# Block sums of v of batch 2: from TensorE products to GpSimd additions of a second load, with the list of steps from entry 270 to 660 in another order

## The chip, the cores and the metric

The kernel runs on one core of one Trainium2 chip. The time is the device time of one execution in microseconds; the median of three runs of the kernel before is 215.75 us (215.53 to 216.22). Differences of less than 0.3% can't be told from none with such runs.

## The reference

Two stages. The first is an attention over q, k, v of shape 4 x 8 x 768 x 64 (batch, head, position, width), in which each position sees its near neighbours and, in place of all the others, one summary per block of 32 positions: the maximum of k and the mean of v.

```python
k_sum = k.reshape(B, H, nb, block, D).max(axis=3)
v_sum = v.reshape(B, H, nb, block, D).mean(axis=3)
scores_l = scale * np.matmul(q, k.transpose(0, 1, 3, 2))      # kept where |i - j| < 16
scores_s = scale * np.einsum('bhsd,bhnd->bhsn', q, k_sum) + np.log(block)
a = softmax(concatenate([scores_l_m, scores_s], axis=-1))
out = np.matmul(a, concatenate([v, v_sum], axis=2))
```

The second is a two-layer network on the 3072 rows that come out (512 wide): h = x @ w_in (to 2048), g = h * clip(h + 3, 0, 6) / 6, y = g @ w_out.

The change concerns `v_sum`, the sums of 32 rows of v, of batch 2 alone.

## The kernel before, in words

**Tiles.** The 3072 rows are eight tiles s = 0 to 7 of 384 rows, two per batch. The *first product* of a tile and of one of 16 column groups ft (`F<s>x<ft>`, L695) is four TensorE products into one of three PSUM banks h0 to h2; ScalarE's relu (L699) and VectorE's gate (L700) turn it into 128 rows of g, and the gate sets the bank free for the third first product behind. The *second product* (`G<s><ts>x..`, L712) multiplies g with w_out in four parts; ScalarE or VectorE copies the result out (L244) and SyncE stores it.

**Attention, batches 1 to 3.** GpSimd issues the loads: k and q in four pieces of 192 KB each (`K<b><g>`, `Q<b><g>`, L336), v in two halves of 384 KB (`V<b>0`, `V<b>2`, L346), and for batches 2 and 3 a halo of v (`H<b>`, L355). Those of batch 2 go into the tile `first`, those of batch 3 into `kraw` and `qraw`. VectorE turns k and q (`w<b><p>`, L458 and L462; a turn reads all four pieces) and takes the block maxima (L470). The scores of a batch are four groups of 48 products (`s<b><u><half>`, L515) into both wide banks S0 and S1, each followed by two exponentials on ScalarE (L523) and two mask products on VectorE (L524). The values (`v<b><half><g>`, L652) need the scores' result, v and the block sums of v.

**Block sums of v** (`u<b+3>`, function `vsum`). For batches 1 and 2 TensorE makes them: 48 products of v with a 0/1 matrix `ind` (L558), a copy into `vs`, and four copies (`vspread2`, L244) that spread them over `vaug`, where the values read them. For batch 3 GpSimd makes them: v is loaded a second time in four pieces (`B3.0` to `B3.3`, `load_blocks`, L582), with the 32 rows of a block side by side in one partition, into the part of `first` that batch 2's k and q have left by then; then nine additions (L564): seven over 128x512 elements, two that halve what is left. The four copies are the same.

**Order.** Nothing is scheduled by the compiler: each engine works through its instructions in the order in which they are recorded, and the recording follows the string `ORDER` (L29 to L87), one entry per step: `u5.0` is step 0 of `vsum(2)`; `:A` and `:D` choose ScalarE or VectorE where both can do it. `Plan.issue` takes each entry in turn, gives it the PSUM bank or buffer that has been free longest, and records it. So an instruction that waits holds up whatever is listed later on its engine.

Of the kernel before, what the change touches and what calls it, by code (L numbers as in the profile page):

```python
# [9 lines left out]
F32 = mybir.dt.float32  # L10
# [29 lines left out]
v410.4:D =1 K12.0 v411.4:A F0x15.2 F0x14.0 F0x9.0 F0x14.1 F0x0.0 F0x9.1 F0x2.0 c.12:A Q1w0.0 F0x2.1 Q1w4.0 F1x4.0 F0x14.2  # L40
F1x4.1 F0x9.2 F1x14.0 w10.0 F1x14.1 F1x2.0 F1x2.1 Q1w1.0 F1x4.2 F0x2.2 F0x2.3 F0x0.1 Q1w2.0 F1x1.0 F1x14.2 F0x2.4 F1x8.0 F1x2.2
F1x1.1 F0x2.5 F1x8.1 F0x12.0 F0x0.2 F0x12.1 F1x1.2 F1x8.2 F0x0.3 F1x15.0 w10.1:A F0x12.2 F0x0.4 F0x0.5 F1x15.1 F1x9.0 F1x15.2
F1x9.1 F1x5.0 F1x9.2 w11.0 F1x5.1 F1x5.2 w10.2 q6.0 w11.2 w11.3:D w10.3:D q6.1:A q7.0 q7.1:A F1x7.0 F1x7.1 w11.1:A F1x7.2
F1x12.0 F1x12.1 F1x12.2 O0.0 G02x0.0 Q1w5.0 Q1w3.0 q4.0 q4.1:A q5.0 q5.1:A F1x6.0 F1x6.1 F1x6.2 O1.0 G02x0.1 s100.0 s100.1
s100.3 F1x3.0 w12.0 F1x11.0 F1x11.1 w13.0 w13.2 F1x3.1 F1x11.2 w12.2 w12.1:D O2.0 G02x0.2 s101.0 s101.1 O3.0 F1x10.0 G02x0.3
G02x0.4:A w13.3:D w13.1:A s101.3 F1x0.0 G00x0.0 G00x0.1 w12.3:D s100.2 s101.2 s100.4 V10.0 h100.0:D F1x10.1 h110.0:A F1x10.2
F1x3.2 s110.0 s110.1 s110.2 s101.4 s110.3 G00x0.2 G00x0.3 G00x0.4:A V12.0 u4.0 h130.0:D h120.0:A F1x0.1 u4.1:D u4.2:A u4.4:D
u4.3:D u4.5:D G02x0.5 G01x0.0 G01x0.1 G01x0.2 s110.4 F1x0.2 h111.0:A v100.0 v100.1 v100.2 h121.0:A v101.0 v101.1 v101.2 G01x0.3
G01x0.4:A K20.0 K21.0 K22.0 K30.0 K23.0 w21.0 F1x13.0 F1x13.1 F1x13.2 v100.3 v100.4:A w20.0 w21.3 G12x0.0 w21.2:A v101.3
v101.4:A V22.0 H2.0 h101.0:A w20.3 G12x0.1 G12x0.2 F2x2.0 F2x2.1 F2x11.0 F2x2.2 F2x11.1 F2x11.2 s111.0 w23.0 s111.3 F2x1.0  # L50
F2x1.1 F2x1.2 F2x3.0 F2x3.1 F2x3.2 F2x15.0 F2x15.1 F2x15.2 Q22.0 w23.3 G12x0.3 s111.1 G12x0.4:A F2x5.0 F2x5.1 h131.0:A F2x5.2
F2x6.0 G10x0.0 s111.2 w22.0 w22.3 s111.4 w23.4:A V20.0 H2.1:A K33.0 F2x13.0 F2x13.1 F2x13.2 G10x0.1 F2x6.1 F2x0.0 F2x0.1 F2x0.2
u5.0 u5.1:A u5.5:A F2x6.2 v110.0 v111.0 v111.1 v111.2 Q30.0 F2x4.0 F2x4.1 F2x4.2 Q21.0 Q23.0 Q20.0 w22.4:A F2x10.0 F2x10.1
F2x10.2 F2x12.0 F2x12.1 w20.1 F2x12.2 w22.2:A v110.1 w21.4:A Q33.0 Q32.0 G10x0.2 G01x0.5 G10x0.3 G10x0.4:A v110.2 F2x8.0 F2x8.1
w21.1 w20.2:A F2x9.0 w20.4:A F2x9.1 F2x9.2 u5.2:D F2x14.0 u5.4:D w23.2:A F2x8.2 v111.3 F2x14.1 v111.4:A G11x0.0 G11x0.1 u5.3:D
w22.1 v110.3 v110.4:A F2x7.0 F2x7.1 G11x0.2 F3x14.0 F3x14.1 F2x14.2 F2x7.2 F3x14.2 s200.0 s200.1 w23.1 w21.5:A s200.3 G11x0.3
F3x9.0 F3x9.1 F3x9.2 F3x8.0 F3x8.1 F3x8.2 F3x13.0 Q31.0 K31.0 s200.4 s200.2 G11x0.4:A G11x0.5 G12x0.5 s210.0 s210.3 s210.4
s210.1 s210.2 F3x4.0 F3x12.0 G22x0.0 F3x13.1 F3x13.2 H3.0 v201.0 K32.0 V32.0 w20.5:D F3x4.1 F3x4.2 V30.0 B3.0 B3.1 B3.2 B3.3
u6.0 u6.1 u6.2 u6.3 u6.4 u6.5 u6.6 u6.7 u6.8 G00x0.5 F3x12.1 v200.0 v200.1 F3x2.0 v201.1 v201.2 v201.3 G22x0.1 F3x0.0 F3x0.1
G22x0.2 G22x0.3 w23.5:A G22x0.4:A F3x12.2 v200.2 v200.3 v201.5 F3x1.0 F3x1.1 F3x1.2 s201.0 w31.0 G20x0.0 v201.4 F3x0.2 F3x2.1  # L60
s201.3 F3x2.2 F3x11.0 s201.1 G20x0.1 F3x5.0 F3x11.1 F3x3.0 F3x5.1 F3x11.2 w30.0 F3x5.2 v201.7 F3x15.0 G20x0.2 F3x15.1 F3x15.2
w30.3 F3x3.1 F3x3.2 w22.5:A w30.4:D s201.4 F3x6.0 F3x6.1 H3.1:A G20x0.3 G20x0.4:A F3x7.0 F3x10.0 G21x0.0 s211.0 F3x7.1 F3x10.1
s201.2 F3x7.2 s211.3 s211.1 F3x10.2 w32.0 F3x6.2 w32.3 s211.4 s211.2 w30.2:A G21x0.1 G21x0.2 G21x0.3 G21x0.4:A u6.12:A u6.11:A
u6.9:A w31.3 v211.0 v201.6 v210.0 v210.1 v210.2 w31.2:D v211.1 v210.3 v211.2 v211.3 G10x0.5 w31.4:D w33.0 G32x0.0 G32x0.1
# [17 lines left out]
F7x2.0 G62x0.1 F7x15.0 F7x2.1 F7x2.2 F7x15.1 F7x15.2 F7x0.0 G62x0.2 F7x0.1 G62x0.3 F7x7.0 F7x7.1 F7x0.2 G71x0.0 G62x0.4:D
G62x0.5 F7x7.2 F7x11.0 F7x11.1 G61x0.0 F7x11.2 F7x14.0 G71x0.1 G71x0.2 G71x256.0 G61x0.1 F7x14.1 F7x14.2 G71x0.3 G71x0.4:A
G72x0.0 G72x0.1 G71x0.5 G41x0.5 G70x0.0 G61x0.2 G61x0.3 G61x0.4:A G52x0.5 G70x0.1 G70x0.2 G72x0.2 G50x0.0 G50x0.1 G61x0.5
G50x0.2 G50x0.3 G72x0.3 G70x0.3 G50x0.4:A G50x0.5 G70x0.4:D G70x0.5 G60x0.0 G60x0.1 G60x0.2 G72x0.4:D G72x0.5 G60x0.3 G71x256.1
G71x256.2 G60x0.4:D G60x0.5 G71x256.3 G71x256.4 G71x384.0 G71x384.1 G71x384.2 G71x384.3 G71x384.4:D G71x384.5
# [76 lines left out]
def kernel(  # L163
# [40 lines left out]
    vrows = first[:].rearrange("p c x -> p (c x)")[:, 0:2 * BLK * D].rearrange("p (h t d) -> p h t d", h=2, t=BLK)  # L204
    quad = first[:].rearrange("p c x -> p (c x)")[:, 2 * BLK * D:2 * BLK * D + 16 * D].bitcast(F32).rearrange("p (h t d) -> p h t d", h=2, t=4)
# [343 lines left out]
    def vsum(b):  # L549
        plan.at(f"u{b + 3}")  # L550
        vs, i = Buf("vs"), b % 2
        if b < B - 1:
# [9 lines left out]
        else:  # L562
            def add(o, x, y):
                nc.gpsimd.tensor_tensor(o, x, y, op=ALU.add)  # L564

            def rows4(n):
                return vrows[:, :, 4 * n:4 * n + 4]
            op("POOL", "badd4", lambda: add(quad[:], rows4(0), rows4(1)), r=[("vb", c) for c in range(NP)], w=["part"], free=["part"])
            for n in range(2, BLK // 4):
                op("POOL", "badd4", lambda n=n: add(quad[:], quad[:], rows4(n)), w=["part"])  # L570
            op("POOL", "badd2", lambda: add(quad[:, :, 0:2], quad[:, :, 0:2], quad[:, :, 2:4]), w=["part"])
            op("POOL", "badd1", lambda: add(vs.slot[:].rearrange("p (h d) -> p h d", h=2), quad[:, :, 0], quad[:, :, 1]), r=["part"], w=[vs])
# [193 lines left out]
    for b in range(1, B):  # L766
# [18 lines left out]
        if b == B - 1:  # L785
            load_blocks(b)
# [53 lines left out]
```

## Time and profile before

| | us |
|---|---|
| median of the runs | 215.75 (215.53 to 216.22) |
| profiled execution, whole | 216.44 |
| its span, from the first to the last instruction | 214.7 |
| TensorE busy | 207.2 |
| VectorE busy | 161.1 |
| ScalarE busy | 137.2 |
| GpSimd busy | 61.5 |

The profiled execution is one more execution, and 0.69 us longer than the median; 1.7 us of it lie outside the span. Lines of the profile name the source line, the engine (PE is TensorE, PEld its weight loads, DVE VectorE, ACT ScalarE, POOL GpSimd, SP SyncE), the operation, the tiles as out<-in, the shape and the count. The rows of a timeline begin with start and duration in us; `[0.42 <-X]` is idle time of the engine before, and what ended it. A row of a group ends with busy time, mean duration in ns, and idle time before.

### The profile page before, as it was taken

To read this page: it belongs to the slowest core of one execution; us is meant where nothing else is said; L and a number is where in the kernel's file an instruction comes from. 1 tells how busy PE (TensorE), PEld (TensorE's weight loads), DVE (VectorE), ACT (ScalarE), POOL (GpSimd) and SP (SyncE) were. 2 spreads that over 40 slices of the span, in tenths; PEclk is the share of its full clock that TensorE was granted. 3 is DMA by queue.
4 is the path that set the end of the run, shared out by engine and by line. 5 is a ranking of instruction groups with operands and counts; after the bars stand their busy time and mean duration, and the time that the engine had idled before them with its cause. 6 is when DMAs were issued, how large, how long until landed. Compare 5 with 4: busy or idle time off the path is not lost.

```text
span 214.7 us, 5971 instructions
## 1 busy us (share of the span) xinstructions
PE 207.2 (97%) x2465; PEld 119.7 (56%) x2492; DVE 161.1 (75%) x311; ACT 137.2 (64%) x270; POOL 61.5 (29%) x79
## 2 busy tenths in 40 slices
PE   7998999999999999999999999999999999999994
PEld 7556566655555565555545555555555555564443
DVE  6886999899799999898899889887865555550021
ACT  3879978887888989765579696566346355520110
POOL 7968258905643237209700000000000000000000
PEclk9999999999999999999999999999999999999999
DMA  5999999999999999990234233113324300113123
GB/s 75 159 151 186 204 188 172 190 203 163 202 162 190 180 133 144 175 229 18 28 39 151 28 39 107 52 17 38 75 37 64 73 3 3 46 52 122 49 81 139
DMA packets 92043, 23.45 MB, mean 109 GB/s; under 512 B 82352, under 2 KB 88880, under 8 KB 92016
## 3 DMA queue, kind: packets, MB, share of 16 engines
q0 software_dynamic: 62608, 15.20, 74.8%
q1 hardware_dynamic: 29264, 7.80, 15.5%
q8 instruction: 19, 0.31, 0.6%
q10 hardware_dynamic: 144, 0.07, 0.1%
q14 instruction: 8, 0.07, 0.1%
HBM read 30.39 MB, written 6.29 MB: 171 GB/s over the span
## 4 chain that ended last, share of the span: by engine, by line
PE 88%; DMA 3%; ACT 2%; issue 2%; POOL 2%; DVE 1%; POOLq 0%
PE h L695 39%; PE o L712 32%; PE h L712 5%; DMA first<-in_q_dram 3%; PE S L652 3%; PE S L515 3%; ACT vaug L244 2%; POOL first L308 1%; PE S L695 1%; PE S L665 1%; PE S L492 1%; PE S L558 1%; PE S L442 1%; PE h L808 1%; DVE vaug L244 0%
## 5 line engine op out<-in xcount | busy, mean ns | idle before, releaser
L695 PE MATMUL h<-x,win 128*128 128x384 bf16 x500 | 91.4, 326 | 0.1
L700 DVE SCALAR_TENSOR_TENSOR g<-r,h 128x384 bf16<-128x384 f32 x125 | 65.8, 547 | 22.5 <-ACT r L699 19.8
L699 ACT ACTIVATE r<-h 128x384 f32<-128x384 f32 x125 | 58.4, 492 | 37.6 <-PE h L695 35.7
L712 PE MATMUL o<-wout,g 128*128 128x512 bf16 x309 | 78.0, 379 | 1.9 <-issue 0.8
L695 PEld LDWEIGHTS <-win 128*128 128x128 bf16 x512 | 48.7, 98 | 35.4
L712 PEld LDWEIGHTS <-g 128*128 128x128 bf16 x416 | 38.7, 98 | 37.4 <-issue 0.3
L523 ACT ACTIVATE at<-S 120x768 bf16<-120x768 f32 x24 | 18.6, 810 | 5.6 <-PE S L515 5.5
L244 ACT COPY ot<-o 128x512 f32<-128x512 f32 x17 | 10.0, 587 | 15.7 <-PE o L712 14.5
L524 DVE TENSOR_TENSOR at<-at,mask 96x768 bf16<-96x768 bf16 x24 | 12.6, 549 | 2.2 <-ACT at L523 1.8
L634 DVE TENSOR_TENSOR xn<-S,rc 128x768 bf16<-128x768 f32 x14 | 13.3, 950 | 0.3
L244 DVE COPY ot<-h 128x512 f32<-128x512 f32 (+1 forms) x3 | 1.6, 554 | 14.3 <-PE h L712 14.3
L346 POOL DMA_DIRECT2D vaug<-in_v_dram x10 | 11.8, 1192 | 0.0
L564 POOL TENSOR_TENSOR first<-first 128x512 f32<-128x512 f32 (+2 forms) x8 | 8.8, 1102 | 9.5 <-DMA first<-in_v_dram 8.9
L712 PE MATMUL h<-wout,g 128*128 128x128 bf16 (+2 forms) x80 | 11.4, 294 | 0.0
L244 ACT COPY vaug<-vaug 32x640 bf16<-32x640 bf16 (+3 forms) x20 | 10.6, 579 | 1.0 <-ACT qT L244 0.7
L470 DVE TENSOR_REDUCE red<-kaug 128x24 bf16<-128x768 bf16 x12 | 11.1, 939 | 0.1
L244 ACT COPY vaug<-vs 24x1536 bf16<-24x1536 bf16 x6 | 8.8, 1468 | 0.1
L808 PE MATMUL o<-idle 128*128 128x64 bf16 (+2 forms) x71 | 7.7, 286 | 1.1 <-DVE idle L290 1.1
L458 DVE STREAM_TRANSPOSE kaug<-kraw 128x768 bf16<-128x768 bf16 x8 | 8.1, 1026 | 0.3 <-PE S L515 0.3
L336 POOL DMA_DIRECT2D kraw<-in_k_dram x8 | 5.7, 724 | 8.4 <-DVE kaug L458 7.1
L652 PEld LDWEIGHTS <-at 120*64 120x64 bf16 x336 | 6.3, 111 | 3.2 <-issue 1.2
L515 PEld LDWEIGHTS <-kaug 32*128 32x128 bf16 x576 | 5.3, 92 | 4.6 <-issue 3.6
(114 smaller groups left out, 193.3 us busy)
## 6 DMA issues: line engine op xcount, KB each, us to landing
out_dram<-ot SPq DMA_DIRECT2D x19, 256.0 KB, 2.3
vaug<-in_v_dram POOLq DMA_DIRECT2D x6, 384.0 KB, 13.6
wout<-in_moe_w_out_dram POOLq DMA_DIRECT2D x4, 512.0 KB, 9.9
win<-in_moe_w_in_dram POOLq DMA_DIRECT2D x3, 512.0 KB, 10.6
kraw<-in_k_dram POOLq DMA_DIRECT2D x8, 192.0 KB, 12.5
x<-y SPq DMA_DIRECT2D x64, 24.0 KB, 2.0
first<-in_k_dram POOLq DMA_DIRECT2D x6, 192.0 KB, 12.7
first<-in_q_dram POOLq DMA_DIRECT2D x6, 192.0 KB, 11.5
```

Source lines behind the costliest of these rows:

```text
L244: {"ACT": nc.scalar.copy, "DVE": nc.vector.tensor_copy, "POOL": nc.gpsimd.tensor_copy}[eng](o, i)
L346: op("POOL", "dma128", lambda: nc.gpsimd.dma_start(out=o[BLK:WIN, a:z, 0:D], in_=rows[:, a:z]), w=[("v", b % 2, c) for c in range(lo, hi)] ...
L470: op("DVE", "max", lambda: nc.vector.tensor_reduce(red.slot[:], w[:, :, BLK:WIN].rearrange("p t (n c) -> p t n c", n=2), axis=AX.X, op=ALU ...
L515: nc.tensor.matmul(X[g // 2].slot[:, g % 2, i * QB:(i + 1) * QB], kaug[2 * u + m][rows, t], qT[rows, 2 * u + m, t * QB:(t + 1) * QB], star ...
L523: op("ACT", "exp", lambda a=a, e=e: nc.scalar.activation(a, X[e].slot[0:KEYS, :, 0:HALF], AF.Exp, scale=scl), r=[X[e]], w=[("at", p, half)])
L524: op("DVE", "masking", lambda m=m: nc.vector.tensor_tensor(m, m, mask[:, low(half):low(half) + HQ].unsqueeze(1).to_broadcast([WIN, 2, HQ, ...
L634: nc.vector.tensor_tensor(o, src[..., 0:D], r.unsqueeze(len(r.shape)).to_broadcast(list(o.shape)), op=ALU.mult)
L652: nc.tensor.matmul(X.slot[64 * c:64 * c + 64, i, m:m + D + 1], a[:, t * QB:(t + 1) * QB], vaug[b % 2][0:KEYS, h, t, 0:D + 1], start=True, ...
L695: nc.tensor.matmul(bank(h)[:, 0:HALF], w_in_sb[:, kt, cols], xt[s].slot[:, kt], start=(kt == 0), stop=(kt == NP - 1))
L699: op("ACT", "relu", lambda: nc.scalar.activation(r.slot[:], bank(h)[:, 0:HALF], AF.Relu, bias=0.5, scale=1.0 / 6.0), r=[h], w=[r])
L700: op("DVE", "gate", lambda: nc.vector.scalar_tensor_tensor(gt[s].slot[:, ft], r.slot[:], 1.0, bank(h)[:, 0:HALF], op0=ALU.min, op1=ALU.mul ...
L712: nc.tensor.matmul(o.slot[:, a:z], gt[s].slot[:, ft, ts * 128:(ts + 1) * 128], w_out_sb[:, ft, a:z], start=(ft == 0), stop=(ft == NFT - 1))
```

## The change

Batch 2's block sums are now made as batch 3's are: by GpSimd, from a second load of v. Since `first` still holds batch 2's k and q at that time, the load goes into a new tile `own`, whose unused rows GpSimd first sets to zero (`Z.0`). The 48 products, their bank and the copy out of it fall away for batch 2. Batch 1 keeps the products.

```diff
+    own = sb([128, 2 * BLK * D + 16 * D], BF16, "own")
+    lent = first[:].rearrange("p c x -> p (c x)")
+    vrows = {b: t[:, 0:2 * BLK * D].rearrange(...) for b, t in ((2, own), (3, lent))}
+    quads = {b: t[:, 2 * BLK * D:2 * BLK * D + 16 * D].bitcast(F32).rearrange(...) for b, t in ((2, own), (3, lent))}
...
     def vsum(b):
-        if b < B - 1:
+        if b < 2:
...
     def load_blocks(b):
+        if b == 2:
+            plan.at("Z")
+            op("POOL", "bzero", lambda: nc.gpsimd.memset(own[:, 0:2 * BLK * D].bitcast(F32), 0.0), w=[("vb", b, c) for c in range(NP)])
         plan.at(f"B{b}")
...
-               w=[("vb", c)], free=[(n, 0, g) for n in ("Kr", "Qr") for g in range(4)], size=48)
+               w=[("vb", b, c)], free=[(n, 0, g) for n in ("Kr", "Qr") for g in range(4)] if b == 3 else (), size=48)
...
-        if b == B - 1:
+        if b > 1:
             load_blocks(b)
```

The list gets twelve more entries, and those from about 270 to 660 stand in another order (the tail from `F4x8.0` on is as before, and so is the order of each engine but GpSimd ahead of `G02x0.0`). One line of it, before and after:

```diff
-F2x6.0 G10x0.0 s111.2 w22.0 w22.3 s111.4 w23.4:A V20.0 H2.1:A K33.0 F2x13.0 F2x13.1 F2x13.2 G10x0.1 F2x6.1 F2x0.0 F2x0.1 F2x0.2
+G10x0.3 v111.1 F2x5.1 F2x14.1 F2x14.2 Q33.0 F2x13.0 G12x0.5 F2x5.2 G10x0.4:A v110.1 u5.0 K33.0 F2x12.1 v111.2 F2x13.1 w20.4:A
```

TensorE, where the values of batch 1's second half begin (`at` are the masked scores, `vaug` v with its block sums, `h` the bank of a first product). Before:

```order
L695 LDWEIGHTS win
L695 MATMUL h_90<-x_99,win 128x384
L558 LDWEIGHTS ind
L558 MATMUL S_89<-vaug_76,ind 32x128
...
L652 LDWEIGHTS at_72
L652 MATMUL S_88<-vaug_77,at_72 64x65
```

After (lines behind the change are eight higher):

```order
L703 LDWEIGHTS win
L703 MATMUL h_91<-x_100,win 128x384
L660 LDWEIGHTS at_74
L660 MATMUL S_90<-vaug_78,at_74 64x65
L660 LDWEIGHTS at_74
```

The 48 pairs on `ind` are gone, and the values follow the first product.

GpSimd, from batch 2's q pieces to the end of its work. Before:

```order
L336 DMA first<-in_q_dram 32x24x128 x3
L336 DMA qraw<-in_q_dram 32x24x128 x3
L336 DMA kraw<-in_k_dram 32x24x128
L355 DMA vaug_77<-in_v_dram 32x95x64
L336 DMA kraw<-in_k_dram 32x24x128
L346 DMA vaug_77<-in_v_dram 64x48x64 x2
L582 DMA first<-in_v_dram 24x2x2048 x4
L564 TENSOR_TENSOR first<-first 128x512 x7
L564 TENSOR_TENSOR first<-first 128x2x128
L564 TENSOR_TENSOR vs_117<-first 128x128
```

After, the first chain of additions, on `own`:

```order
L567 TENSOR_TENSOR own<-own 128x512
L339 DMA kraw<-in_k_dram 32x24x128
L567 TENSOR_TENSOR own<-own 128x512
L339 DMA qraw<-in_q_dram 32x24x128
L567 TENSOR_TENSOR own<-own 128x512 x3
L339 DMA kraw<-in_k_dram 32x24x128
L567 TENSOR_TENSOR own<-own 128x512
L349 DMA vaug_78<-in_v_dram 64x48x64
L567 TENSOR_TENSOR own<-own 128x512
L590 DMA first<-in_v_dram 24x2x2048 x2
L567 TENSOR_TENSOR own<-own 128x2x128
L567 TENSOR_TENSOR vs_119<-own 128x128
```

and the second, on `first`:

```order
L590 DMA first<-in_v_dram 24x2x2048 x2
L339 DMA kraw<-in_k_dram 32x24x128
L358 DMA vaug_78<-in_v_dram 32x95x64
L567 TENSOR_TENSOR first<-first 128x512
L339 DMA qraw<-in_q_dram 32x24x128
L567 TENSOR_TENSOR first<-first 128x512 x6
L349 DMA vaug_78<-in_v_dram 64x48x64
L567 TENSOR_TENSOR first<-first 128x2x128
L567 TENSOR_TENSOR vs_118<-first 128x128
L339 DMA qraw<-in_q_dram 32x24x128
```

All loads stood ahead of the additions before. Now thirteen loads stand between additions or behind them, the last of them a piece of batch 3's q.

More of the change, by code (lines that the diff above doesn't have):

```diff
@@ L45 @@
[L45 to L48, printed above, removed]
@@ L53 @@
[L53 to L56, printed above, removed]
@@ L57 @@
[L57 to L64, printed above, removed]
@@ L82 @@
[L82 to L86, printed above, removed]
+F1x12.0 F1x12.1 F1x12.2 O0.0 G02x0.0 F1x10.0 F1x10.1 Q1w5.0 F1x10.2 Q1w3.0 O1.0 q4.0 q5.0 G02x0.1 F1x3.0 F1x6.0 q5.1:A q4.1:A
@@ new lines @@
+G20x0.1 F3x7.0 F3x0.0 w31.0 s201.3 F3x5.2 v201.4 v201.5 s201.1 s211.0 F3x7.1 u6.5 u6.6 F3x0.1 s211.3 F3x7.2 G20x0.2 s211.4
+G20x0.3 F3x0.2 F3x2.0 w32.0 F3x11.0 F3x1.0 G20x0.4:A G21x0.0 w31.3 F3x2.1 F3x2.2 v201.6 V30.0 u6.7 G21x0.1 G21x0.2 w31.2:A
+s201.2 G21x0.3 s211.1 v201.7 F3x6.0 w30.0 F3x11.1 F3x1.1 F3x11.2 u6.8 s211.2 G21x0.4:A s201.4 u6.11:A F3x10.0 v211.0 F3x1.2
+v210.0 F3x15.0 w32.3 F3x6.1 w30.3 F3x10.1 F3x6.2 u6.9:A F3x15.1 v211.1 F3x10.2 G32x0.0 G32x0.1 w33.0 F4x4.0 v210.1 u6.12:A
+F3x15.2 w32.2:A Q30.0 G32x0.2 G32x0.3 G32x0.4:A F4x15.0 v210.2 F4x14.0 v211.2 F4x4.1 F4x14.1 w30.4:D F4x15.1 G30x0.0 G30x0.1
@@ new lines @@
+F5x7.2 v311.1 F5x8.0 F5x8.1 F5x8.2 F5x10.1 F5x10.2 G40x0.2 F5x12.0 G40x0.3 G40x0.4:A G42x0.5 F5x15.0 F5x11.0 v310.3 v311.2
+v311.3 v311.7 F5x11.1 G32x0.5 G41x0.0 G41x0.1 G41x0.2 F5x11.2 F5x15.1 F5x15.2 F6x14.0 F5x12.1 F5x12.2 F6x14.1 F6x14.2 F6x12.0
+F6x12.1 F6x12.2 F6x9.0 F6x9.1 F6x9.2 G41x0.3 G41x0.4:A F6x10.0 F6x10.1 F6x7.0 F6x4.0 F6x4.1 F6x10.2 G52x0.0 F6x4.2 F6x7.1
+F6x7.2 F6x8.0 F6x8.1 F6x1.0 F6x8.2 F6x1.1 F6x1.2 F6x0.0 F6x0.1 F6x0.2 G52x0.1 F6x3.0 F6x11.0 F6x11.1 G52x0.2 F6x3.1 F6x3.2
+G52x0.3 G52x0.4:D F6x5.0 F6x5.1 F6x11.2 F6x2.0 F6x2.1 F6x5.2 F6x2.2 G51x0.0 F6x13.0 F6x13.1 F6x6.0 F6x15.0 G51x0.1 v311.6
@@ L87 @@
+G71x0.1 G71x0.2 G71x256.0 G61x0.1 F7x14.1 F7x14.2 G71x0.3 G71x0.4:A G72x0.0 G72x0.1 G71x0.5 G41x0.5 G70x0.0 G61x0.2 G61x0.3
+G61x0.4:A G52x0.5 G70x0.1 G70x0.2 G72x0.2 G50x0.0 G50x0.1 G61x0.5 G50x0.2 G50x0.3 G72x0.3 G70x0.3 G50x0.4:A G50x0.5 G70x0.4:D
+G70x0.5 G60x0.0 G60x0.1 G60x0.2 G72x0.4:D G72x0.5 G60x0.3 G71x256.1 G71x256.2 G60x0.4:D G60x0.5 G71x256.3 G71x256.4 G71x384.0
+G71x384.1 G71x384.2 G71x384.3 G71x384.4:D G71x384.5
 """
@@ L203 @@
     kraw, qraw = ([sb([128, NP * NB, BLK], BF16, f"{n}raw"), first[:, i * NP * NB:(i + 1) * NP * NB]] for i, n in enumerate("kq"))
-    vrows = first[:].rearrange("p c x -> p (c x)")[:, 0:2 * BLK * D].rearrange("p (h t d) -> p h t d", h=2, t=BLK)
-    quad = first[:].rearrange("p c x -> p (c x)")[:, 2 * BLK * D:2 * BLK * D + 16 * D].bitcast(F32).rearrange("p (h t d) -> p h t d", h=2, t=4)
+    own = sb([128, 2 * BLK * D + 16 * D], BF16, "own")
+    lent = first[:].rearrange("p c x -> p (c x)")
+    vrows = {b: t[:, 0:2 * BLK * D].rearrange("p (h t d) -> p h t d", h=2, t=BLK) for b, t in ((2, own), (3, lent))}
+    quads = {b: t[:, 2 * BLK * D:2 * BLK * D + 16 * D].bitcast(F32).rearrange("p (h t d) -> p h t d", h=2, t=4) for b, t in ((2, own), (3, lent))}
     at = [sb([128, 2, S], BF16, f"at{p}") for p in range(NP)]
@@ L564, in add @@
                 nc.gpsimd.tensor_tensor(o, x, y, op=ALU.add)
+            quad = quads[b]
             def rows4(n):
-                return vrows[:, :, 4 * n:4 * n + 4]
-            op("POOL", "badd4", lambda: add(quad[:], rows4(0), rows4(1)), r=[("vb", c) for c in range(NP)], w=["part"], free=["part"])
+                return vrows[b][:, :, 4 * n:4 * n + 4]
+            op("POOL", "badd4", lambda: add(quad[:], rows4(0), rows4(1)), r=[("vb", b, c) for c in range(NP)], w=[("part", b)])
             for n in range(2, BLK // 4):
-                op("POOL", "badd4", lambda n=n: add(quad[:], quad[:], rows4(n)), w=["part"])
-            op("POOL", "badd2", lambda: add(quad[:, :, 0:2], quad[:, :, 0:2], quad[:, :, 2:4]), w=["part"])
-            op("POOL", "badd1", lambda: add(vs.slot[:].rearrange("p (h d) -> p h d", h=2), quad[:, :, 0], quad[:, :, 1]), r=["part"], w=[vs])
+                op("POOL", "badd4", lambda n=n: add(quad[:], quad[:], rows4(n)), w=[("part", b)])
+            op("POOL", "badd2", lambda: add(quad[:, :, 0:2], quad[:, :, 0:2], quad[:, :, 2:4]), w=[("part", b)])
+            op("POOL", "badd1", lambda: add(vs.slot[:].rearrange("p (h d) -> p h d", h=2), quad[:, :, 0], quad[:, :, 1]), r=[("part", b)], w=[vs])
         for c in range(NP):
@@ L582, in load_blocks @@
             op("POOL", "dmarows", lambda c=c: nc.gpsimd.dma_start(
-                out=vrows[32 * c:32 * c + NB].rearrange("p h t d -> p h (t d)"),
+                out=vrows[b][32 * c:32 * c + NB].rearrange("p h t d -> p h (t d)"),
                 in_=v[b, 2 * c:2 * c + 2].rearrange("h (n t) d -> n h (t d)", t=BLK)),
-               w=[("vb", c)], free=[(n, 0, g) for n in ("Kr", "Qr") for g in range(4)], size=48)
+               w=[("vb", b, c)], free=[(n, 0, g) for n in ("Kr", "Qr") for g in range(4)] if b == 3 else (), size=48)
     xt, ys = {}, {}
```

55 lines of the change are left out of this document (31 added, 24 removed).

## Prediction

> **What bounds the kernel now.** I read the page's totals first, then the busy time by stretches, then the waits in the stretch that is laid out anew (44 to 121 us), then single instructions.
>
> ```profile
> span 214.7 us, 5971 instructions
> PE 207.2 (97%) x2465; PEld 119.7 (56%) x2492; DVE 161.1 (75%) x311; ACT 137.2 (64%) x270; POOL 61.5 (29%) x79
> DMA  5999999999999999990234233113324300113123
> 60.00:80.00 20.00, 19.66 (x288) 11.75 (x290) 19.28 (x32) 17.56 (x34) 7.25 (x10) 1.00 1.95 169
> 80.00:100.00 20.00, 19.68 (x249) 11.05 (x254) 18.66 (x33) 13.89 (x32) 9.54 (x11) 1.00 1.39 151
> 100.00:121.00 21.00, 20.72 (x239) 11.18 (x242) 19.27 (x36) 16.10 (x29) 5.74 (x6) 1.00 0.32 60
> PE o L712 <- issue: 0.6, 4, 0.2
> DVE g L700 <- ACT r L699: 2.6, 6, 0.7
> ```
>
> The columns of the stretches are TensorE, its weight loads, VectorE, ScalarE and GpSimd. TensorE works 60.06 of the 61 us from 60 to 121; what it waits for between 44 and 121 us adds up to 0.6 us. So TensorE's work is the time, at a granted clock of 1.00. But VectorE is close behind: 57.21 of the same 61 us, and 96% from 60 to 80. It waits 2.6 us for ScalarE. The DMA row is full to slice 18 (97 us). So whatever leaves TensorE is gain at once, as long as neither VectorE nor a load becomes late by more than the little that is spare.
>
> **What leaves TensorE.** The block sums of batch 2 in the timeline, with what stands around them:
>
> ```profile
> 75.54 0.81 PE L695 MATMUL h<-x,win 128*128 128x384 bf16 x4
> ...
> 76.28 0.68 PEld L558 LDWEIGHTS <-ind 96*32 96x32 bf16 x48 [0.32 <-DMA qraw<-in_q_dram]
> 76.29 0.85 PE L558 MATMUL S<-vaug,ind 96*32 96x128 bf16 x48
> ...
> 76.64 1.47 DVE L700 SCALAR_TENSOR_TENSOR g<-r,h 128x384 bf16<-128x384 f32 x3
> 77.07 0.90 PEld L652 LDWEIGHTS <-at 120*64 120x64 bf16 x48
> ...
> 77.19 0.27 ACT L244 CAST vs<-S 128x128 bf16<-128x128 f32 x1 [0.25 <-PE S L558]
> ...
> 78.01 2.12 PE L695 MATMUL h<-x,win 128*128 128x384 bf16 x12
> ```
>
> From the first weight load of the sums to that of the values behind them: 77.07 - 76.28 = 0.79 us. All of it goes, with ScalarE's copy of the sums (0.27 us, hidden). The short idle of the weight loads ahead of such a group (0.32 us here) stays: it belongs to the change from a first product to a group of another tile shape. The old order has 14 such changes in the stretch and the new one 14 as well, since the values now follow a first product directly. The number of products, transposes, scores and values on TensorE is the same. So the term is **-0.8 us**. What the other order makes of the 0.94 us that TensorE does not work between 60 and 121 I put at nothing, with bounds: all of it may go, or as much may come. One new wait I can name: the second score group of batch 1 now has one first product fewer between it and the group before, whose two banks it takes over.
>
> **GpSimd's side.** It gets a memset, four loads and nine adds, ahead of the nine it has.
>
> ```profile
> L564 POOL TENSOR_TENSOR first<-first 128x512 f32<-128x512 f32 (+2 forms) x8 | 8.8, 1102 | 9.5 <-DMA first<-in_v_dram 8.9
> L336 POOL DMA_DIRECT2D first<-in_q_dram x4 | 2.9, 717 | 4.7 <-DMA vaug<-in_v_dram 4.3 <-issue 0.3
> L346 POOL DMA_DIRECT2D vaug<-in_v_dram x4 | 5.4, 1342 | 0.0
> L582 POOL DMA_DIRECT2D first<-in_v_dram x4 | 2.6, 678 | 1.3 <-DVE qT L462 1.3
> L252 POOL MEMSET ident<- 128x128 bf16 x1 | 0.2, 224 | 0.0
> 59.79 1.12 POOL L336 DMA_DIRECT2D qraw<-in_q_dram  x1 [0.75 <-DMA first<-in_k_dram]
> 65.36 0.71 POOL L336 DMA_DIRECT2D first<-in_q_dram  x1 [2.69 <-DMA vaug<-in_v_dram]
> 78.65 1.33 POOL L355 DMA_DIRECT2D vaug<-in_v_dram  x1 [5.35 <-PE S L652]
> 96.23 9.36 POOL L564 TENSOR_TENSOR first<-first 128x512 f32<-128x512 bf16 x8 [8.95 <-DMA first<-in_v_dram]
> 105.67 0.46 POOL L564 TENSOR_TENSOR vs<-first 128x128 bf16<-128x128 f32 x1
> DMA to landing us min/median/max: 11.1/11.1/11.1
> DMA to landing us min/median/max: 6.3/6.3/6.3
> first<-in_v_dram POOLq DMA_DIRECT2D x4, 192.0 KB, 9.3
> ```
>
> The first landing row is of the load issued at 65.36, the second of the halo load of batch 3 (issued at 78.65, after GpSimd had waited 5.35 us and the queue had run nearly empty). The memset has 2048 elements a row against 128 for 0.224 us: between 0.2 and 3.6 us, beside a full queue, free.
>
> Fourth new load landed: before, the load of 65.36 landed at 76.5, and by then the queue had brought all k, q and v pieces of batch 2 and three pieces of batch 3; now the fourth new load has ahead of it 960 KB less (one v half of 384 KB, three pieces of 192) and, itself included, 768 KB more. At 169 GB/s that is 75.3 us; if the new loads, whose rows are long, take only the 0.6 us a piece at which the old ones were issued, 73.0. Adds: a chain of nine is 96.23 to 106.13 = 9.9 us. Between them the new order puts three loads of 0.72, one of 1.34 and two of 0.68: 4.9 us. So the sums of batch 2 stand at 87.8 to 90.1. They are needed when VectorE spreads them, and the next chain goes on behind: two more issues, a landing of 6.3 to 9.3 us, 9.9 us of adds with loads of 0.72 and 1.34 between: end of the sums of batch 3 at 107 to 112, then the last q load of batch 3, landing at 113 to 121. The needs:
>
> ```profile
> 91.03 1.21 DVE L700 SCALAR_TENSOR_TENSOR g<-r,h 128x384 bf16<-128x384 f32 x2 [0.55 <-ACT r L699]
> 112.71 0.59 ACT L244 COPY ot<-o 128x512 f32<-128x512 f32 x1 [0.49 <-PE o L712]
> 120.65 1.02 DVE L462 STREAM_TRANSPOSE qT<-qraw 128x768 bf16<-128x768 bf16 x1
> ```
>
> The first spread of batch 2 now stands behind the gate of 91.03 (done at 91.58), with 0.5 us less VectorE work ahead by the order and the mean durations of the groups: 91.1, or 90.3 where TensorE is 0.8 earlier. ScalarE spreads batch 3 behind the output copy of 112.71, with 3.5 us less ahead: about 109.8. The first turn of q of batch 3, at 120.65, has 2.9 us less ahead and TensorE 0.8 earlier: 117.0. For the first chain I take the middle, 89.0. Behind it I take the short landing, because the DMA row is far from full after slice 18: 89.0 + 0.7 + 6.3 = 96.0 for the last load, + 9.9 + 0.72 + 1.34 = 107.9 for the sums of batch 3, + 6.3 = 114.2 for the q load. So the three needs are met with 1.3, 1.9 and 2.8 us to spare, and the cost taken is **0**; at the upper ends the last one is 4.4 us late.
>
> **VectorE's side.** It has the same number of instructions and nearly the same work, in 0.8 us less: of its 3.8 us of idle time from 60 to 121, 3.0 are left. What is spare before TensorE notices is read above: the three gates that begin at 76.64 end at 77.18 to 78.11, and the products that take their banks start at 78.01, 78.66 and 79.31: 0.8 to 1.2 us. Cost taken: 0.
>
> GpSimd and VectorE may also stop each other. The trace shows a little of it:
>
> ```profile
> 84.87 1.12 DVE L244 COPY vaug<-vs 24x1536 bf16<-24x1536 bf16 x2
> L582 POOL DMA_DIRECT2D first<-in_v_dram x4: 603/609/892, 84.6 to 86.7; - x4
> L524 DVE TENSOR_TENSOR at<-at,mask 96x768 bf16<-96x768 bf16 x16 | 8.3, 548 | 0.5 <-ACT at L523 0.3
> 107.46 1.01 DVE L524 TENSOR_TENSOR at<-at,mask 96x768 bf16<-96x768 bf16 x2
> ```
>
> One of four load issues takes 0.89 instead of 0.61 us, the one beside VectorE's copies: 0.3 us. Beside the adds (96 to 106) VectorE had no mask product; those at 107.46 come after them. In the new order two mask products fall into the second chain, none into the first. If each stands through a whole add of 1.16 us, that is 2.3 us of VectorE. The Trainium skill ("SBUF — State Buffer", section "Who interferes with whom") states just this: a VectorE instruction with two SBUF inputs contends with a GpSimd instruction that reads SBUF, and the later one waits for the whole of the other. By that rule the sum would be up to 1.3 us higher (2.3 less the 1.0 spare); no row here shows it for adds.
>
> **The sum.** The profiled execution took 216.44 us, 1.7 beyond its span; the median of the runs shown is 215.75. Both lose the same 0.8: 215.64 for a run like the profiled one, and **215.0** for the median, which I give.
>
> **The rivals.**
> - *VectorE takes over.* For it: 96% in one stretch. Against: its waits are for ScalarE, whose work falls. The 0.8 us come back as waits for gates: 215.4 to 216.2, say 215.8. Chance 0.23.
> - *GpSimd's chain is late.* For it: one q load that was issued at 59.8 us is now GpSimd's last instruction but the end, behind eighteen adds and the landings they wait for. VectorE, in order, stands at the turn of q, with the gates behind it. At the upper ends 4.4 us late, less 1.0 spare, 3.4 reach TensorE: 215.0 + 3.4 = 218.4. It costs something from 3.8 us beyond my value on (2.8 + 1.0), and turns the sign past the measure from 5.2. Chance 0.13.
> - *Masks stand behind adds*, as above: 216.3. Chance 0.05.
> - *The new layout also takes the rest of TensorE's idle time*: -0.8 - 0.9 gives 214.1. Chance 0.12.
>
> **How the numbers follow.** The forecast (214.7 to 215.4) has 0.47. A measurement of this kernel tells about 0.3%, 0.65 us: below 215.10 counts as faster, above 216.40 as slower. Faster: 0.12 and three quarters of 0.47, so 0.47. Slower: nearly all of 0.13 and a little of the rest, 0.14. The same: 0.39. The range 214.2 to 216.7 leaves out half of the best case and most of the late chain.
>
> **What would show it.** In the profile after: no 48 products on the indicator of batch 2; TensorE's waits between 44 and 121 us still under 1 us, and the last first product of tile 3 about 0.8 us earlier. Right on GpSimd: the first chain ends by 90 us, the second by 109, and no VectorE or ScalarE wait names GpSimd or a q load. Wrong: a VectorE wait on the q load of batch 3 near 117 us; a ScalarE wait on the sums near 110; mask products of more than 1 us between 100 and 108; or VectorE without idle time and TensorE's products waiting for gates.

## The result, and the profile after

| | before | after |
|---|---|---|
| median of the executions, us | 215.93 (215.53 to 216.61, 20) | 218.02 (215.98 to 221.79, 20) |
| ratio, with its 95% interval | | 1.0061 (1.0042 to 1.0081) |
| profiled execution, us | 216.44 | 217.09 |
| its span, us | 214.7 | 215.4 |
| TensorE busy, us | 207.2 | 205.4 |

Slower by 0.6%, or 1.3 us, where 0.8 us less was forecast. The ratio leaves out the seven slowest executions of the changed kernel, of which more at the end; the profiled one has a granted clock of 1.0.

The page of the changed kernel: totals, and TensorE's row of slices.

```profile
span 215.4 us, 5887 instructions
PE 205.4 (95%) x2416; PEld 118.3 (55%) x2444; DVE 159.5 (74%) x310; ACT 135.8 (63%) x270; POOL 74.7 (35%) x93
PE   7998999999999999999995999999999999999994
```

TensorE does less work, as it should (2416 products on record against 2465), but the row has a 5 in slice 22 (113 to 118 us). Before, that slice was full:

```profile
PE   7998999999999999999999999999999999999994
```

The waits of TensorE between 44 and 121 us (total, times, longest), which before came to 0.6 us:

```profile
PE h L703 <- DMA x<-y: 2.5, 1, 2.5
PE o L720 <- issue: 0.6, 4, 0.2
PE S L660 <- DVE vaug L247: 0.2, 1, 0.2
```

One new wait of 2.5 us, and it is for a transfer that the prediction never mentions. In the timeline, the weight loads (PEld) of the first second product, of tile 3's last group, of tile 4's first product, and of the place from which the two lists are alike again:

```profile
43.35 0.69 PEld L720 LDWEIGHTS <-g 128*128 128x128 bf16 x4
...
111.67 1.55 PEld L720 LDWEIGHTS <-g 128*128 128x128 bf16 x8
116.16 0.45 PEld L703 LDWEIGHTS <-win 128*128 128x128 bf16 x4 [2.93 <-issue]
...
121.37 1.94 PEld L703 LDWEIGHTS <-win 128*128 128x128 bf16 x12
```

TensorE's products of tile 4 in the same timeline, with the wait ahead of them:

```profile
116.19 0.81 PE L703 MATMUL h<-x,win 128*128 128x384 bf16 x4 [2.46 <-DMA x<-y]
```

The same weight loads in the kernel before (tile 4's first product aside):

```profile
44.18 0.69 PEld L712 LDWEIGHTS <-g 128*128 128x128 bf16 x4
...
113.78 1.19 PEld L712 LDWEIGHTS <-g 128*128 128x128 bf16 x7
...
120.71 1.94 PEld L695 LDWEIGHTS <-win 128*128 128x128 bf16 x12
```

And there, tile 4's first products:

```profile
117.25 1.95 PE L695 MATMUL h<-x,win 128*128 128x384 bf16 x11
```

Read these in pairs. At 44 us the changed kernel is 0.83 us ahead, ahead of anything that the change touches: that is how two executions differ (over the twelve kernels traced here, of both orders, this load starts between 43.24 and 44.62 us). At the last group of tile 3 it is 113.78 - 111.67 = 2.11 us ahead, so 1.28 us were gained in between: the forecast's 0.8 and some 0.5 more. This pair can't put the 0.5 down to the other order: one of the kernels below ("The same loss made in the kernel before", the loads alone), in which TensorE has the order of before, does the same stretch in 69.20 us, the kernel before in 69.60. Then comes the wait, and from 121 us on the kernel is 121.37 - 120.71 = 0.66 us behind. Gain of 1.28, loss of 2.77, net 1.49 us later; the ratio says 1.3.

**What the transfer is.** A tile's x, which its first products read, is put together by SyncE: VectorE turns the values (`y`, L679), and 16 small transfers of 24 KB move it into place (`x<-y`, L685; L677 before). The instructions of that line between 99 and 118 us are the 16 moves of tile 4. Before:

```profile
L677 SPq DMA_DIRECT2D x<-y x16: 617/618/1710, 100.2 to 111.3; - x16
DMA to landing us min/median/max: 2.0/2.0/3.4
```

After, with who waited for them:

```profile
L685 SPq DMA_DIRECT2D x<-y x16: 617/620/1446, 101.0 to 112.2; - x16
  PEld L703: 2.9, 1
  PE h L703: 2.5, 1
DMA to landing us min/median/max: 2.0/3.3/5.3
```

The first row gives the issue of one (ns, least, median, most) and the starts of the first and the last. One is issued every 0.7 us, so the last leaves SyncE at 111 to 112 us in both kernels. What differs is the landing: 2.0 us in the middle before, 3.3 after. For the wait only the last one counts: issued at 111.3 us it landed 2.8 us later, near 114.1, before; issued at 112.2 it landed 3.8 us later, near 116.0, after. So of the 1.9 us between them 0.9 is a later issue and 1.0 a longer landing. And the first product that needs it stood at 117.25 us before, 3 us behind the last landing (114.1 in the trace); now, listed behind two parts of tile 3's last group instead of four, and with TensorE 1.28 us ahead, it could start at about 113.7 us.

**GpSimd's side.** Its two chains in the timeline of the changed kernel (first and last of the first chain, first of the second, the last v half, the end of the second chain, the last q piece):

```profile
73.61 1.34 POOL L567 TENSOR_TENSOR own<-own 128x512 f32<-128x512 bf16 x1 [5.15 <-DMA own<-in_v_dram]
...
87.46 0.46 POOL L567 TENSOR_TENSOR vs<-own 128x128 bf16<-128x128 f32 x1
...
96.71 1.15 POOL L567 TENSOR_TENSOR first<-first 128x512 f32<-128x512 bf16 x1 [5.58 <-DMA first<-in_v_dram]
...
106.05 1.36 POOL L349 DMA_DIRECT2D vaug<-in_v_dram  x1
...
108.25 0.46 POOL L567 TENSOR_TENSOR vs<-first 128x128 bf16<-128x128 f32 x1
108.64 0.73 POOL L339 DMA_DIRECT2D qraw<-in_q_dram  x1
```

On VectorE, the first spread of batch 2 and the first turn of q of batch 3:

```profile
91.28 0.56 DVE L247 COPY vaug<-vs 24x1536 bf16<-24x1536 bf16 x1
...
117.35 1.00 DVE L465 STREAM_TRANSPOSE qT<-qraw 128x768 bf16<-128x768 bf16 x1
```

Nothing here is late: sums of batch 2 at 87.9 us, those of batch 3 at 108.7, and neither the spread at 91.28 nor the turn of q at 117.35 has idle time ahead of it. But see the last two loads, a v half of 384 KB at 106.05 and a q piece of 192 KB at 108.64. Before, they were issued at 82.0 and 59.8 us, ahead of the moves; now they are issued among them (101 to 112 us), and land 6.9 and 5.7 us later, near 113.0 and 114.3. The moves issued up to 106.6 us land in 2.0 to 2.9 us, those issued from 107.2 on in 3.8 to 5.3.

### The profile page after: what moved, and what is told of

Read it like the earlier page. It is cut to its first block, busy times and chain, and to the rows that moved or that the text cites. A ratio compares the mean times of both kernels' runs of the same rounds, so it can differ in the third digit from the quotient of the medians.

```text
span 215.4 us, 5887 instructions
## 1 busy us (share of the span) xinstructions
PE 205.4 (95%) x2416; PEld 118.3 (55%) x2444; DVE 159.5 (74%) x310; ACT 135.8 (63%) x270; POOL 74.7 (35%) x93
## 4 chain that ended last, share of the span: by engine, by line
PE 83%; SPq 5%; DMA 4%; ACT 2%; issue 2%; DVE 2%; POOL 0%; POOLq 0%
PE h L703 37%; PE o L720 28%; PE h L720 5%; SPq L685 5%; PE S L518 2%; PE S L660 2%; DMA first<-in_k_dram 2%; DMA x<-y 2%; PE o L816 1%; DVE vaug L247 1%; ACT vaug L247 1%; PE S L703 1%; PE S L673 1%; PE S L495 1%; PE h L816 1%
## 5 line engine op out<-in xcount | busy, mean ns | idle before, releaser
L703 PE MATMUL h<-x,win 128*128 128x384 bf16 x500 | 91.1, 326 | 2.5 <-DMA x<-y 2.5
L527 DVE TENSOR_TENSOR at<-at,mask 96x768 bf16<-96x768 bf16 x24 | 13.6, 584 | 2.0 <-ACT at L526 1.6
L567 POOL TENSOR_TENSOR own<-own 128x512 f32<-128x512 f32 (+2 forms) x8 | 9.1, 1135 | 5.4 <-DMA own<-in_v_dram 5.1
L247 ACT COPY vaug<-vaug 32x640 bf16<-32x640 bf16 (+2 forms) x18 | 9.3, 575 | 0.7 <-ACT qT L247 0.7
```

The source lines that it names most:

```text
L247: {"ACT": nc.scalar.copy, "DVE": nc.vector.tensor_copy, "POOL": nc.gpsimd.tensor_copy}[eng](o, i)
L527: op("DVE", "masking", lambda m=m: nc.vector.tensor_tensor(m, m, mask[:, low(half):low(half) + HQ].unsqueeze(1).to_broadcast([WIN, 2, HQ, ...
L703: nc.tensor.matmul(bank(h)[:, 0:HALF], w_in_sb[:, kt, cols], xt[s].slot[:, kt], start=(kt == 0), stop=(kt == NP - 1))
```

## The experiments

The theory: *moves against loads, and an early product*. Two loads that GpSimd now issues late share the DMA engines with SyncE's moves of tile 4's x, and tile 4's first product is listed where it can no longer stand a late landing. The rivals: the GpSimd additions themselves (through memory or through VectorE), or the other order on TensorE. All ratios are to the kernel before, on the same chip.

### The two loads ahead

GpSimd issues both ahead of the second chain.

```diff
-v201.0 H3.0 F3x14.2
+v201.0 H3.0 V30.0 Q30.0 F3x14.2
...
-v201.6 V30.0 u6.7
+v201.6 u6.7
...
-w32.2:A Q30.0 G32x0.2
+w32.2:A G32x0.2
```

> The last v half and the last q piece of batch 3 are issued ahead of the second chain of additions instead of inside and behind it; all else as in the changed kernel. Theory 'moves': the 16 transfers that bring tile 4's x together land late because these two loads run beside them (last landing 115.9 us, 3.8 us after its issue, where 2.0 is usual); then the last one lands near 114.2, TensorE's wait ahead of tile 4's first product falls from 2.8 to about 1.0 us, and the time falls by 1.8 us against the changed kernel. Rival 'place': the first product merely stands too early in TensorE's order; then the landing and the wait stay within 0.3 us of what they were. Rival 'additions': GpSimd's additions themselves hold up the other engines; then nothing changes either.

Measured: 215.94 us (214.56 to 216.96), ratio 0.9993 (0.997 to 1.0016). The 16 moves:

```profile
L685 SPq DMA_DIRECT2D x<-y x16: 611/618/1097, 101.5 to 112.1; - x16
DMA to landing us min/median/max: 2.0/2.1/4.9
```

TensorE's wait for them, between 44 and 121 us:

```profile
PE h L703 <- DMA x<-y: 0.2, 1, 0.2
```

The same additions, the same moves issued at the same time: with the loads out of the way they land in 2.1 us in the middle, not 3.3, and the wait falls from 2.5 to 0.2 us. The last move, issued at 112.1 us, lands 2.0 us later; those that take up to 4.9 us are the first ones. Neither rival fits: 'place' expected the landing and the wait as they were, 'additions' expected no change.

### The first product later

Its place is behind four parts again.

```diff
-G32x0.1 w33.0 F4x4.0 v210.1
+G32x0.1 w33.0 v210.1
...
-G32x0.3 G32x0.4:A
+G32x0.3 F4x4.0 G32x0.4:A
```

> Only the first product of tile 4 that TensorE waits at is listed two second-product parts later (1.7 us of work). Theory 'moves' and rival 'place' both: the wait falls from 2.8 to 1.1 us and the time by 1.7 us against the changed kernel. Rival 'additions': the wait moves with the product or turns up elsewhere, and the time stays within 0.5 us of the changed kernel.

Measured: 215.87 us (214.79 to 217.65), ratio 0.9997 (0.9971 to 1.0022). The moves still land late:

```profile
DMA to landing us min/median/max: 2.0/3.2/5.2
```

But TensorE waits little for them:

```profile
PE h L703 <- DMA x<-y: 0.3, 1, 0.3
```

So either half of the theory, undone, brings the time back to that of before (by the ratios, 1.5 and 1.4 us less than the changed kernel). Neither brings the forecast's 0.8 us, and their executions scatter over 2.4 and 2.9 us. A likely reason is that both still stand at the edge of the wait: the traced executions, which show 0.2 and 0.3 us of it, are 0.7 and 0.9 us shorter than the medians. An execution of median length was not traced.

### Both

> Both edits. If they act on the same wait from its two sides, no wait is left there, and the time is 2.8 us under the changed kernel: about 214.5 us, 0.6 to 0.7% under the kernel before, which is the forecast's 0.8 us for the products that fell away, and a little more. If the two edits act on the same 1.7 us, a wait of 1 us stays. Rival 'additions': no gain over the changed kernel.

Measured: 214.95 us (214.54 to 215.23, 6 executions), ratio 0.995 (0.9934 to 0.9967). TensorE goes from tile 3's last group into tile 4 without a gap:

```profile
112.82 3.19 PE L720 MATMUL o<-wout,g 128*128 128x512 bf16 x14
115.84 1.46 PE L703 MATMUL h<-x,win 128*128 128x384 bf16 x8
```

This kernel beats both, by 1.0 us the one before, and its executions lie within 0.7 us.

### The wait filled

One entry, `~10`, has TensorE make ten products over 512 columns on constants behind `G32x0.1`, into a bank that is free; nobody reads them.

```diff
-G32x0.0 G32x0.1 w33.0 F4x4.0
+G32x0.0 G32x0.1 ~10 w33.0 F4x4.0
```

> In the changed kernel's wait, TensorE makes ten products of 512 columns (2.2 us) on constants, which nothing reads. The wait is only filled, so the execution at a granted clock of 1.00 keeps its time within 0.3 us. Theory 'clock': half of the changed kernel's executions show a granted clock of 0.98 to 0.99 because TensorE idles there; with the filler all show 1.00, and the executions at 218 us and above vanish. Rival 'other cause of the clock': as many executions as before show it.

Measured: 217.51 us (216.70 to 219.41), ratio 1.008 (1.0049 to 1.0111).

```profile
113.37 2.32 PE L816 MATMUL h<-idle 128*128 128x512 bf16 x10
115.80 0.81 PE L703 MATMUL h<-x,win 128*128 128x384 bf16 x4
```

The filler takes the place of the wait, and the time stays, by the ratios (1.008 against 1.0061), what it was. So the time is set by when the moves land, not by TensorE's work. All eight executions had a granted clock of 1.0, as the theory has it (see the last section). But the executions at 218 us and above did not vanish, as it also has it: three of the eight took 218.05 to 219.41 us at a clock of 1.0, and what made them long is not known.

### The same loss made in the kernel before

First the two loads alone: in the kernel before, without any GpSimd sums of batch 2, GpSimd issues them behind its only chain. The halo step that reads the v half (`H3.1`) moves behind `F4x8.2`.

```diff
-v111.2 Q30.0 F2x4.0
+v111.2 F2x4.0
...
-F3x4.2 V30.0 B3.0
+F3x4.2 B3.0
...
-u6.8 G00x0.5
+u6.8 V30.0 Q30.0 G00x0.5
```

> The kernel before, with nothing changed but its last v load and one q load of batch 3, which GpSimd now issues behind its additions (about 106 and 108 us), as in the changed kernel; the halo step that reads that v comes later too. Theory (moves of x against loads, and an early product): the last move of tile 4's x lands about 1.8 us later, near 115.9 instead of 114.1 us, but the first product that reads it is reached only at 117.0, so the time is that of before, 216.0 +- 0.4, and no wait on x<-y appears. Rival (a late load costs by itself, by its needs or by the shared engines): 1 to 2 us longer.

Measured: 216.19 us (215.40 to 217.59), ratio 1.0016 (0.9993 to 1.0039). Then the product too, ahead of tile 3's last group:

```diff
-w31.4:D w33.0 G32x0.0 G32x0.1
+w31.4:D w33.0 F4x14.0 G32x0.0 G32x0.1
...
-G32x0.4:A F4x14.0 F4x14.1
+G32x0.4:A F4x14.1
```

> The kernel e5, with tile 4's first product moved ahead of the four parts of the second product that stood before it (about 3.5 us earlier on TensorE). Theory: reached at about 113.6 us, it waits for the last move near 115.9, so a wait of about 2.3 us on x<-y appears and the time is 218.0 to 218.6, in a kernel that has no GpSimd sums of batch 2. Rival (the sums of batch 2 on GpSimd, through memory or engine contention, make the loss): 216.0 to 216.5.

Measured: 217.89 us (217.80 to 219.81, 4 executions), ratio 1.0112 (1.0077 to 1.0147). The moves' landings with the loads alone:

```profile
DMA to landing us min/median/max: 2.0/3.4/6.2
```

Tile 4's first products in that kernel, without a wait:

```profile
117.06 2.11 PE L696 MATMUL h<-x,win 128*128 128x384 bf16 x12
```

With the product early too, the landings:

```profile
DMA to landing us min/median/max: 2.0/3.6/6.3
```

And the product, in that kernel's timeline:

```profile
115.34 0.81 PE L696 MATMUL h<-x,win 128*128 128x384 bf16 x4 [1.40 <-DMA x<-y]
```

The late loads make the moves late in this kernel as well (3.4 us against 2.0), and that costs nothing as long as the product stands at 117; with the product early, a loss of 1.1% is there without a single addition for batch 2. The early product without the late loads was not run in this kernel. The wait was 1.4 us where 2.3 was expected: the product was reached at 113.9 rather than 113.6, and the last move landed earlier than in the changed kernel. Another 0.6 us went at 94 us in this execution: a mask took 1.54 us beside the first of batch 3's additions, and TensorE waited for it. So not all of this loss is the moves'.

### The products put back

The kernel of "Both" with 48 products on batch 1's v, of the same shape and at the old place. Their bank is read by nobody.

```diff
+        if b == 2:
+            T = Buf("S")
+            def again():
+                ...
+            op("PE", "sums4", again, r=[...], w=[T])
...
-F2x12.0 w20.3 v111.0
+F2x12.0 w20.3 u5.13 v111.0
```

> The kernel e3 (loads ahead, product later), with 48 more products put back on TensorE ahead of the values of batch 1's second half, where the kernel before has the sums of batch 2. They work on batch 1's v and write a bank that nobody reads; batch 2's sums still come from GpSimd. Theory (the products' term of 0.79 us is right): e3 plus 0.8, that is 215.7 (215.4 to 216.0), ratio about 0.998 to the kernel before. Rival (most of e3's gain is the other order, and the products lay in idle time): 215.0 to 215.3.

Measured: 216.05 us (215.63 to 216.75), ratio 0.9999 (0.9984 to 1.0015). The weight loads of the products and of the values behind them:

```profile
75.60 0.68 PEld L590 LDWEIGHTS <-ind 96*32 96x32 bf16 x48 [0.32 <-issue]
76.39 0.84 PEld L670 LDWEIGHTS <-at 120*64 120x64 bf16 x48
```

From one weight load to the other 0.79 us, the prediction's term to the digit. By the ratios (0.9999 against 0.995) it is 1.1 us, uncertain by some 0.5 us, so the two agree. With the products back the time is that of the kernel before, within 0.15%: nearly the whole gain of "Both" is the products, and if the other order gains or loses anything there, it is too little to tell.

### The sums alone, and the order alone

Two tries to take the change apart, both of which made waits of their own. First batch 2's sums by GpSimd in the order of before; the additions and loads stand where GpSimd has time for them, the four spreads (three others stood between `F2x9.2` and `w22.1`) behind them.

```diff
-F2x0.2 u5.0 u5.1:A u5.5:A F2x6.2
+F2x0.2 F2x6.2
...
-F3x9.1 F3x9.2 F3x8.0 F3x8.1 F3x8.2
+F3x9.1 F3x9.2 u5.12:D F3x8.0 F3x8.1 u5.10:A F3x8.2 u5.9:D
...
-s200.2 G11x0.4:A
+s200.2 u5.11:D G11x0.4:A
```

> Batch 2's sums by GpSimd as in the changed kernel, but TensorE, VectorE and ScalarE keep the order of before; only the four spreads stand 4 to 12 us later, and GpSimd's loads of batch 3 are arranged round the two chains with the last one issued before the second chain. Theory: no wait ahead of tile 4's first product, and the 0.8 us of the forecast come out: 215.2 (214.9 to 215.6). Rival (the product's 0.8 us are taken back by VectorE or by contention with the additions, whatever the order): 215.8 to 216.5.

Measured: 220.65 us (218.73 to 221.27, 6 executions), ratio 1.0205 (1.0169 to 1.0241). TensorE's waits between 44 and 121 us:

```profile
PE S L660 <- DVE vaug L247: 0.9, 1, 0.9
PE o L720 <- ACT ot L247: 0.8, 1, 0.8
PE S L660 <- DVE at L527: 0.4, 1, 0.4
```

The traced execution is the shortest of the six. No wait for a move, but waits for a spread, for an output copy that stood behind a halo step on ScalarE, and for a mask. A second try gave the spreads, the values and, not shown, the loads and that halo step other places:

```diff
-w23.1 ... F3x9.1 F3x9.2 u5.12:D ... u5.10:A F3x8.2 u5.9:D ... s200.2 u5.11:D
+w23.1 u5.12:D ... F3x9.1 u5.10:A F3x9.2 u5.9:D ... F3x8.2 u5.11:D ... s200.2
...
-G22x0.0 ... v201.0 ... v200.0 v200.1 F3x2.0 ... G22x0.1
+G22x0.0 G22x0.1 ... F3x2.0 v201.0 v200.0 v200.1
```

> The kernel e7, in which TensorE waited 1.2 us for a spread on VectorE and 1.0 us behind a halo step of batch 3 that stood on ScalarE waiting for a v load: the spreads are each placed one or two instructions earlier, the values of batch 2's first half one part of a second product later, the halo step of batch 3 behind tile 4's first products, and the halo load between the first additions. Theory (those two waits, not the sums by GpSimd as such, made e7 slow): both go, and 215.2 to 216.2 is left. Rival (the sums by GpSimd cost by themselves in this order): 217 or more.

Measured: 218.01 us (216.93 to 218.57, 5 executions), ratio 1.008 (1.0052 to 1.0109); in the same stretch:

```profile
PE h L703 <- DVE g L708: 1.5, 3, 0.6
```

The two waits are gone and gates are late instead. The expectation failed. In the old order the spreads stood between 77 and 87 us; sums from GpSimd are ready at 89.0 and 88.0 us in these two kernels, so the four spreads fall into the stretch up to the values at 95, among masks and gates, and both kernels had waits there. That suggests that the change needs another order, which it brings; it isn't shown, since whether some order near the old one would do was not found.

The order alone: the changed kernel's list, with batch 2's sums as 48 products again. Not shown are the entries of the second load and the additions, which go, and the spreads, which keep their places. The halo step `H2.1`, which the products read, moves up.

```diff
-u5.0 K33.0 F2x12.1 v111.2 F2x13.1 w20.4:A
-u5.1 F2x8.0 G11x0.0
+K33.0 F2x12.1 v111.2 F2x13.1 w20.4:A
+H2.1:A F2x8.0 u5.0 G11x0.0
```

> The changed kernel's order, with batch 2's sums on TensorE again (48 products, as before; no second load, no first chain of additions). Theory: the moves of x still land near 115.9 us beside the two late loads, and tile 4's first product still waits; since it is reached 0.8 us later, the wait is that much shorter, about 2.0 us, and the time is that of the changed kernel, 217.5 to 218.3. Rival (the chains of additions make the loss): 216.0 or less.

Measured: 221.05 us (220.58 to 221.99, 4 executions), ratio 1.023 (1.0202 to 1.0258). The expectation failed here too, and for another cause. VectorE in the timeline:

```profile
95.88 1.42 DVE L525 TENSOR_TENSOR at<-at,mask 96x768 bf16<-96x768 bf16 x1
97.31 1.88 DVE L245 COPY vaug<-vs 24x1536 bf16<-24x1536 bf16 x1
99.20 1.02 DVE L245 COPY qT<-qT 128x16 bf16<-128x16 bf16 x1
```

GpSimd beside it, three additions that took 3.64 us in the first chain of the changed kernel:

```profile
97.58 4.12 POOL L565 TENSOR_TENSOR first<-first 128x512 f32<-128x512 f32 x3
```

And TensorE's values of batch 2:

```profile
100.74 0.57 PE L653 MATMUL S<-vaug,at 120*64 120x65 bf16 x24 [2.63 <-DVE at L525]
```

A mask, a spread and a small copy took 4.3 us together where they take 0.55, 0.56 and 0.16 by themselves, and TensorE waited 2.6 us for the next mask: batch 3's additions began 1 us earlier than in the changed kernel and the spreads later, so they met. TensorE also waited 1.1 us for `H2.1` at 80 us, and its granted clock fell to 0.50 for some 3 us behind the wait for the mask (see the last section). No wait for a move came; tile 4's first product was reached only at 120.9 us. So the order can't be priced by this run.

## Why the prediction was wrong

- **The step that failed** is the one on the other order: "What the other order makes of the 0.94 us that TensorE does not work between 60 and 121 I put at nothing, with bounds: all of it may go, or as much may come." A wait of 2.5 us came, past the bound. The prediction looked for waits on banks, spreads and q, and named one (two banks of a score group); SyncE's moves of x, on which every first product of a new tile depends, stand in none of its steps. The wait that it named did not come: no row of TensorE's waits in that stretch names a score group.
- **The last loads** were judged by their needs only: whether the q piece would land before 117.0. It did. What they would do to other transfers was not asked; "because the DMA row is far from full after slice 18" was taken as a reason for their own short landing. There it held: the q piece landed 5.7 us after its issue, near 114.3 (114.2 forecast). But 24 KB moves with someone waiting were slowed all the same, from 2.0 to 3.3 us in the middle (5.3 at most). "The two loads ahead" showed this half, "The first product later" the other, and the pair in the kernel before made the wait from both.
- **The term of 0.8 us was right**: 0.79 us in "The products put back". Undoing the two causes together gives the forecast's 215.0 (214.95 measured; by the ratio -1.1 us, with 0.7 to 1.4 as its interval).
- **GpSimd's chain was right**: sums of batch 2 at 87.9 (89.0 taken, 87.8 to 90.1 as bounds), sums of batch 3 at 108.7 (107.9), first spread 91.28 (91.1), turn of q 117.35 (117.0). The rival that priced lateness there, 218.4, gives nearly the median measured, by luck: the mechanism was another, since no VectorE or ScalarE wait names GpSimd or a q load.
- **VectorE** did not take over in the changed kernel, but gates were late in one of the two kernels with the order of before ("The sums alone").
- **Masks behind adds**: two of them met GpSimd in the second chain, as the order said, one an addition and one the issue of a load. In VectorE's timeline of the changed kernel:

```profile
102.77 1.08 DVE L527 TENSOR_TENSOR at<-at,mask 96x768 bf16<-96x768 bf16 x1
...
106.47 0.87 DVE L527 TENSOR_TENSOR at<-at,mask 96x768 bf16<-96x768 bf16 x1
```

So the sign of being wrong that was named, a mask of more than 1 us between 100 and 108, did show. But the two took 0.85 us more than two at 0.55, less than the 1.0 spare, and no wait in TensorE's list above names a mask. The rule of the Trainium skill that the prediction weighed ("SBUF — State Buffer", section "Who interferes with whom") is borne out most plainly by the order-alone run above, in which a mask took 1.42 us beside an addition. The copies behind it, held up as well, have one input, and the rule as the prediction gives it, for two inputs, doesn't speak of them.

## What to carry to other kernels

When an order is laid out anew, list for each tile what feeds its first step, small transfers on SyncE too, and how far behind the last landing that step stands: a step that had 3 us to spare has none left when it is moved up by two parts (1.7 us) on an engine that is 1.3 us ahead. A load that is moved late is to be asked not only when it is needed but what else is being moved then. And a gain upstream of such a wait is worth nothing until the wait is gone: here 1.28 us were gained and 2.77 lost at one instruction.

## What the runs showed of the hardware

- Moves of 24 KB that SyncE issues land in 2.0 us alone and in 3.3 to 3.6 us in the middle, 5.3 to 6.3 at most, while loads of 384 and 192 KB from GpSimd run. That is not all that slows them: in the kernel before the first two and the last three of the sixteen took 2.8 to 3.4 us with no load from GpSimd in flight, for a reason not found. The Trainium skill ("DMA: Bandwidth & Descriptors", section "Issuing engines are not separate DMA queues") says that transfers of all engines interleave on the same 16 DMA engines; these landings agree.
- The granted clock was 0.983 to 0.992 in ten of the changed kernel's 20 executions, which took 218.3 to 221.8 us; the other ten, at 0.999 or 1.0, took 215.98 to 217.71, in the middle 217.01, which is still 1.1 us above the kernel before. With the wait filled by products it was 1.0 in all of eight, and in the kernels without the wait (loads ahead, product later, both) 0.998 to 1.0 in all of 30. That TensorE's idle time brings the lower clock on fits these counts. One trace shows it happen, that of the order-alone kernel (mean granted clock 0.992). Its page has a slice at 0.7 (99 to 105 us):

```profile
PEclk9999999999999999997999999999999999999999
```

Asked for by shorter stretches, the trace gives 1.00 up to 101 us, 0.91 from 101 to 102, 0.50 from 102 to 105, 0.89 from 105 to 106 and 1.00 from there on: the granted clock was halved for some 3.4 us, which costs 1.7, just behind its wait of 2.6 us (which ended at 100.74). Why it follows such a wait in one execution and not in another is open: of this kernel's four executions only this one had it. It also came in four of six executions of the first "sums alone" kernel, in one of four of the kernel before with late loads and early product, and in one of 18 of the kernel before that ran beside these.
- The executions of the two kernels whose wait is nearly gone scatter over 2.4 and 2.9 us (12 each); those of "The products put back" over 1.1 (12) and of the kernel before over 1.7 (25). That the landings vary from one execution to the next would explain the difference; it isn't shown, since only one execution of each was traced, and the kernel before with the late loads alone, whose traced execution has no wait for a move, scatters over 2.2 us (10).
